# Recurrence loads with three and four buffers in place of five, and one load moved

## Chip, cores, metric

One core of a Trainium2 chip runs the whole program. The metric is device time in microseconds of one execution. Of the kernel before there are three timed runs and one profiled execution.

## What is computed

Three stages, each reading what the one before it wrote. Everything is float32 at the interface.

```python
def _attn_ref(r, k, v, w, u):            # (4, 8, 768, 48) each; w, u (8, 48)
    ...
    for t in range(S):
        kt, vt, rt = (k[:, :, t], v[:, :, t], r[:, :, t])
        cur = np.einsum('bhd,bhe->bhde', u[None] * kt, vt)
        y[:, :, t] = np.einsum('bhd,bhde->bhe', rt, state + cur)
        state = w[None, :, :, None] * state + np.einsum('bhd,bhe->bhde', kt, vt)
def _moe_ref(x, w_skip, w_gate, w1, w2):  # x: (3072, 384), 8 experts, hidden 1024
    ...                                   # tokens with x @ w_skip > 0 go to their best expert
    out[do_compute] = xc + gate_w * (relu(xc @ w1[e]) @ w2[e])
def _moe2_ref(x, phi, w1, w2):            # soft slots: 8 experts with 4 slots each
    ...
```

The change lies in the loads of the first stage, the recurrence.

## The kernel before

The recurrence is done in chunks: 768 steps are 6 chunks of 128, and a tile is one chunk of one of the 4 batches, all 8 heads. There are 24 tiles; tile j is chunk j // 4 of batch j % 4. Within a tile the recurrence is matmuls: scores of keys against queries (`scores`, L656), the scores times the values (`av`, L753, in two halves, the second of which is followed by a copy to `yt`, L758), the state's part (`inter`, L734), and the update of the state (`upd`, L679). The loop at L1024 runs over i, and tile i's scores stand beside the `av` of tile i - 1 and the transposes of tile i - 2.

Two loads feed a tile, both issued on the queue of SP (SyncE) by `load(j)`:

- `rk` (L514): r and k with the head dimension on the partitions, 112 partitions of 4 KB. Its readers are the three products of `prep(j)`: two on DVE (VectorE) at L635 and L636, one on POOL (GpSimd) at L638 (`pd`). The buffers `rkb` are a list of NRK = 5 fixed tiles; tile j uses number j modulo NRK.
- `kv` (L519): k and v with time on the partitions, 128 partitions of 3 KB. Its readers are `prepk(j)` on POOL (L644, the product `kt`, for tiles 0 to 19), then TensorE in `upd(j)` (L679, which reads `kt` and v) and in `av(j)` (L753). The tile `kvt` comes from a pool with five buffers in turn. A load into a buffer waits until the last reader of its former tile is done, which is the second half of `av`.

`prep(i + 1)` and `prepk(i + 1)` are issued in pass i, after the scores of tile i. The engines follow an order written out by hand: every engine, SP too, takes its instructions in the order of the program, so a load that waits holds all that stands behind it on SP. In pass i that is `load(i + 3)`, then from pass 20 to 22 two loads of expert weights each (`wload`, L966 and L968, 768 KB each), and every fourth pass a store of x (`stored`, L809); the last three stores come after the loop. The loads 0 to 2 are issued before the loop (L521 to L626), load 3 at the top of pass 0, ahead of `decays()`, `warm`, `prep(0)` and `prepk(0)`.

After the loop the routing of the tokens is finished, and POOL gathers the tokens of the first expert from the x in HBM with `idg` as the index (`gload`, L1197). The expert stage (`mm1` L1266 to L1269, `mm2` L1291 to L1293) follows, then the slots.

Of the kernel before, what the change touches and what calls it, by code (L numbers as in the profile page):

```python
# [8 lines left out]
F32 = mybir.dt.float32  # L9
# [10 lines left out]
P = 128  # L20
NC_ = S // P
NT = B * NC_
DM = H * D
# [451 lines left out]
def tile_main(ctx, tc, rk, kv, wu, wcat, phi, w1, w2, v1, v2, r_in, k_in, v_in, w_in, u_in, wcn, out, dbg=None, force=False):  # L475
# [9 lines left out]
    wk = ap.enter_context(tc.tile_pool(name="wk", bufs=2))  # L485
# [4 lines left out]
    PE_, DVE_, ACT_, POOL_, SP_ = (mybir.EngineType.PE, mybir.EngineType.DVE, mybir.EngineType.Activation, mybir.EngineType.Pool, mybir.EngineType.SP)  # L490
    mst = ExitStack()
    mst.enter_context(tc.manual_schedule(engines={PE_, DVE_, ACT_, POOL_, SP_}))
    NRK = 5
    ones = fp.tile([P, P], BF16, name="ones")
    nc.vector.memset(ones, float(E))

    def warm(n, w=P):

        wp = ps.tile([P, 2, 4 * P], F32, tag="y", name="wp")[:, 0, 0 : 4 * w]
        for _ in range(n):  # L500
            nc.tensor.matmul(wp, ones, ones[:, 0:w].rearrange("p (o n) -> p o n", o=1).to_broadcast([P, 4, w]), start=True, stop=True)  # L501

    warm(NWARM, 48)
    rkb = [kp.tile([PR, 2, 4, P], F32, name=f"rkb{i}") for i in range(NRK)]
    wt = kp.tile([PR, 2, 4], F32, name="wt")
# [4 lines left out]
    def load(j, first=True, last=True):  # L510
        c, b = divmod(j, B)
        if first:
            t = T[j] = {"rk": rkb[j % NRK]}
            nc.sync.dma_start(out=t["rk"], in_=rk[c, b])  # L514
        if not last:
            return
        t = T[j]
        t["kv"] = wk.tile([P, 2, DM], F32, tag="kvt", bufs=5, name=f"kvt{j}")
        nc.sync.dma_start(out=t["kv"], in_=kv[c, b])  # L519

    load(0, last=False)  # L521
    load(1, last=False)
    load(0, first=False)
    wcs = fp.tile([PR, 4, 64], F32, name="wcs")
    nc.scalar.dma_start(out=wcs, in_=wcat)
# [87 lines left out]
    def decays():  # L613

        pkp = ps.tile([P, 4, 128], F32, tag="r", name="pkp")
        for p in range(4):
            nc.tensor.transpose(pkp[:, p, 0:PR], pks[:, p, :], ident[:PR, :PR])
        to, fr = pktok.rearrange("t (p f) d -> t p f d", f=2), pkp.rearrange("t p (g d) -> t p g d", d=64)
        nc.scalar.copy(to[:, 2:4], fr[:, 2:4, :, 0:D])
        for g in range(2):  # L620
            nc.scalar.copy(to[:, 0:2, 1 - g], fr[:, 0:2, g, 0:D])
# [8 lines left out]
    def prep(j):  # L630
        t = T[j]
        rkt = t["rk"]
        rks = wk.tile([PR, 2, 4, P], F32, tag="rks", bufs=3, name=f"rks{j}")
        t["rs"], t["ks"] = rks[:, 0], rks[:, 1]
        nc.vector.tensor_mul(rks[:, 0], rkt[:, 0], prt)  # L635
        nc.vector.tensor_mul(rks[:, 1], rkt[:, 1], pkt)  # L636
        t["pd"] = wk.tile([PR, 4, P], F32, tag="pd", name=f"pd{j}")
        nc.gpsimd.tensor_mul(t["pd"], rkt[:, 0], rkt[:, 1])  # L638

    def prepk(j):  # L640
        t = T[j]
        if j < NT - B:
            t["kt"] = wk.tile([P, DM], F32, tag="kt", name=f"kt{j}")
            nc.gpsimd.tensor_mul(t["kt"], t["kv"][:, 0], pktok.rearrange("t h d -> t (h d)"))  # L644
# [377 lines left out]
    pa = Banks(u=[(ps, "t", 1)])  # L1022
    if True:
        for i in range(NT):  # L1024
            if i + 3 < NT:
                load(i + 3)
            rc, rb = divmod(i - 5, B)
            rok = 0 <= rc < NC_ - 1
            if i == 0:
                decays()  # L1030
                warm(5, 48)
                prep(0)
                prepk(0)
                for hf in range(2):
                    r0 = 64 * hf
                    nc.vector.tensor_copy(usel[r0 : r0 + D, :, hf : hf + 1], wt[r0 : r0 + D, 1, :].rearrange("p (a o) -> p a o", o=1))
# [318 lines left out]
    if True:  # L1355
# [4 lines left out]
        for n in range(NS + 1):  # L1360
# [12 lines left out]
            f = e - 1  # L1373
# [300 lines left out]
```

## Time and profile before

| | us |
|---|---|
| three timed runs | 348.92, 350.14, 354.14 |
| their median | 350.14 |
| the profiled execution | 348.07 |
| its span (first to last instruction) | 346.3 |
| mean granted clock of TensorE, share of full | 0.967 |

The profiled execution is the one that the rows below describe; what lies around its span is 1.8 us. PE is TensorE's matmuls, PEld its weight loads, SPq the queue of DMA issues on SP. A busy PE is not PE at its peak, since matmuls overlap. Times in rows are microseconds from the start of the span; a line number is that of the kernel before.

### The profile page before, as it was taken

The numbers are of one execution on the slowest core, as the hardware profiler recorded it, in microseconds if no ns is written. First come the engines' busy times: TensorE is split into PE (matmuls) and PEld (weight loads), VectorE is DVE, ScalarE is ACT, GpSimd is POOL, SyncE is SP. The second block draws the span as 40 slices with busy tenths as digits, with TensorE's granted clock in tenths as the row PEclk, the third lists the DMA queues.
The fourth block names the chain that finished last, engine by engine and source line by source line (L and its number), as shares of the span: only waits on it lengthen the run. The fifth ranks groups of instructions, "written<-read, shape, count | busy, mean of one in ns | idle before, by whom it ended". The sixth has DMA issues, their size and how long they took to land.

```text
span 346.3 us, 10440 instructions
## 1 busy us (share of the span) xinstructions
PE 321.4 (93%) x4326; PEld 263.9 (76%) x4326; DVE 226.1 (65%) x510; ACT 159.5 (46%) x353; POOL 139.8 (40%) x181
## 2 busy tenths in 40 slices
PE   8699998999998999999999999999999999999950
PEld 8477776767775782999999999998999998534540
DVE  6637676896969865776675848575676845226850
ACT  3235454444543463554645546464645543121360
POOL 3939685776844544804324232525224002200000
PEclk9969999999999998999999999999999999899995
DMA  7976667684879944899788787878866749779096
GB/s 233 287 220 190 187 189 255 199 269 141 279 191 310 387 163 158 266 310 315 252 288 303 239 281 255 263 257 296 294 197 215 254 124 377 256 268 324 10 338 210
DMA packets 45735, 85.29 MB, mean 246 GB/s; under 512 B 3838, under 2 KB 26672, under 8 KB 45680
## 3 DMA queue, kind: packets, MB, share of 16 engines
q1 hardware_dynamic: 43024, 80.63, 70.8%
q0 software_dynamic: 2128, 3.74, 3.9%
q8 instruction: 36, 0.59, 0.7%
q10 hardware_dynamic: 528, 0.16, 0.2%
q14 instruction: 19, 0.16, 0.1%
HBM read 74.49 MB, written 10.10 MB: 244 GB/s over the span
## 4 chain that ended last, share of the span: by engine, by line
PE 79%; DVE 12%; issue 3%; ACT 2%; POOL 1%; ACTq 0%; DVEq 0%
PE yp L1291 7%; PE yp L1292 6%; PE yp L1293 6%; PE hp L1266 6%; PE hp L1269 6%; PE hp L1267 6%; PE yp L753 4%; PE ehp L216 4%; PE sc L656 3%; PE lgt L837 3%; PE ud L679 3%; PE trp L764 3%; PE yp L734 2%; PE wp L501 2%; PE ud L666 2%
## 5 line engine op out<-in xcount | busy, mean ns | idle before, releaser
L1266 PE MATMUL hp<-xhl,wa 128*128 128x240 f32 x192 | 46.1, 282 | 0.2 <-issue 0.2
L1291 PE MATMUL yp<-wb,hh 128*128 128x384 f32 x128 | 45.2, 353 | 0.0
L1004 DVE TENSOR_TENSOR wa<-w,wa 128x768 fp32r<-128x768 f32 x32 | 30.5, 955 | 22.4 <-ACT wa L1016 22.3
L1267 PE MATMUL hp<-xhl,wa 128*128 128x240 f32 x192 | 44.6, 275 | 0.0
L1292 PE MATMUL yp<-wb,hh 128*128 128x384 f32 x128 | 43.0, 336 | 0.0
L1293 PE MATMUL yp<-wb,hl 128*128 128x384 f32 x128 | 42.9, 335 | 0.0
L1197 POOL DMA_INDIRECT xg<-x_d,idg x16 | 19.9, 1242 | 51.9 <-DVE x L1299 38.1
L638 POOL TENSOR_TENSOR pd<-rkb 112x512 f32<-112x512 f32 x24 | 31.1, 1295 | 18.6 <-PE ud L666 15.3
L1321 POOL DMA_INDIRECT lt_d<-lsr,ids x16 | 17.7, 1106 | 50.2 <-ACT xhl L1256 28.3
L1266 PEld LDWEIGHTS hp<-xhl,wa 128*128 128x128 f32 x192 | 36.2, 189 | 0.5 <-ACT dsbv L135 0.5
L1267 PEld LDWEIGHTS hp<-xhl,wa 128*128 128x128 f32 x192 | 36.2, 189 | 0.0
L714 DVE COPY_PREDICATED at<-ih,ud 128x512 f32<-128x512 int32 x24 | 17.7, 738 | 26.0 <-ACT us L695 16.5
L1004 DVE TENSOR_TENSOR wb<-w,wb 128x768 fp32r<-128x768 f32 x32 | 30.5, 953 | 2.1 <-ACT wb L1016 1.7
L1016 ACT CAST wb<-w 128x768 fp32r<-128x768 f32 x32 | 26.8, 838 | 9.5 <-PE yp L1293 5.5
L753 PE MATMUL yp<-at,kvt 64*48 64x64 f32 (+3 forms) x800 | 27.7, 250 | 1.0 <-DVE at L714 0.4
L1276 ACT ACTIVATE hh<-hp 128x480 fp32r<-128x480 f32 x32 | 18.3, 572 | 22.2 <-PE hp L1269 20.0
L1277 DVE SCALAR_TENSOR_TENSOR hl<-hp,hh 128x480 fp32r<-128x480 f32 x32 | 20.9, 654 | 9.7 <-ACT hh L1276 9.2
L1016 ACT CAST wa<-w 128x768 fp32r<-128x768 f32 x32 | 26.9, 840 | 0.0
L1291 PEld LDWEIGHTS yp<-wb,hh 128*128 128x128 f32 x128 | 24.0, 188 | 3.6 <-issue 3.5
L1269 PE MATMUL hp<-xhl,wa 128*128 128x240 f32 x192 | 26.7, 275 | 0.0
L656 PE MATMUL sc<-rks 48*64 48x128 f32 (+1 forms) x768 | 22.1, 252 | 4.5 <-DVE at L705 2.3
L753 PEld LDWEIGHTS yp<-at,kvt 64*48 64x48 f32 (+1 forms) x800 | 22.2, 125 | 5.3 <-issue 1.6
(346 smaller groups left out, 697.1 us busy)
## 6 DMA issues: line engine op xcount, KB each, us to landing
w<-in_w_dram SPq DMA_DIRECT2D x32, 768.0 KB
v<-in_v_dram SPq DMA_DIRECT2D x29, 768.0 KB
rkb<-in_rk_dram SPq DMA_DIRECT2D x24, 448.0 KB
kvt<-in_kv_dram SPq DMA_DIRECT2D x24, 384.0 KB
x_d<-x SPq DMA_DIRECT2D x5, 768.0 KB
out_dram<-ob SPq DMA_DIRECT2D x5, 768.0 KB
x<-in_v_dram SPq DMA_DIRECT2D x2, 768.0 KB
x_d<-x SPq DMA_DIRECT2D x2, 384.0 KB
```

The lines of the kernel that those rows point to most:

```text
L638: nc.gpsimd.tensor_mul(t["pd"], rkt[:, 0], rkt[:, 1])
L656: nc.tensor.matmul(sc[c0 : c0 + HT, g, blocks(p, z), :], ks[r0 : r0 + D, p, HT * z : HT * z + HT], rs[r0 : r0 + D, p, HT * z :], start=Tru ...
L753: nc.tensor.matmul(d, kvt[s0 : s0 + HT, 1, h * D : h * D + m], w, start=(c == ph == z == 0), stop=(ph == z == 1))
L1004: nc.vector.tensor_sub(lv, sl, hv.bitcast(F32))
L1016: nc.scalar.copy(hv, sl)
L1266: nc.tensor.matmul(hp[:, f, 0:ROOM], hi[:, k, fs], xh[:, k, 0:ROOM], start=(k == 0 and f == 0), stop=False)
L1267: nc.tensor.matmul(hp[:, f, 0:ROOM], lo[:, k, fs], xh[:, k, 0:ROOM], start=False, stop=False)
L1269: nc.tensor.matmul(hp[:, f, 0:ROOM], hi[:, k, fs], xl[:, k, 0:ROOM], start=False, stop=(k == 2 and f == 1))
L1277: nc.vector.scalar_tensor_tensor(l, p, 0.0, h.bitcast(F32), op0=ALU.max, op1=ALU.subtract)
L1291: nc.tensor.matmul(YP[e][bl], hh[:, f, bs], hi[:, f, :], start=st, stop=False)
L1292: nc.tensor.matmul(YP[e][bl], hh[:, f, bs], lo[:, f, :], start=False, stop=False)
L1293: nc.tensor.matmul(YP[e][bl], hlo[:, f, bs], hi[:, f, :], start=False, stop=en)
```

## The change

NRK goes from 5 to 3, the pool's buffers for `kvt` from 5 to 4, and load 3 moves from the top of pass 0 to behind `prep(0)` and `prepk(0)`, which read tile 0. The other loads stay where they are. Since `load(i + 3)` stands at the top of pass i, the `rk` of tile i + 3 takes the buffer that `prep(i)` read in the pass before, and its `kv` takes the buffer of tile i - 1, whose last reader, `av(i - 1)`, comes later in the same pass.

```diff
-    NRK = 5
+    NRK = 3
...
-        t["kv"] = wk.tile([P, 2, DM], F32, tag="kvt", bufs=5, name=f"kvt{j}")
+        t["kv"] = wk.tile([P, 2, DM], F32, tag="kvt", bufs=4, name=f"kvt{j}")
...
         for i in range(NT):
-            if i + 3 < NT:
+            if 0 < i < NT - 3:
                 load(i + 3)
...
                 prep(0)
                 prepk(0)
+                load(3)
```

## Rows read from the trace of the kernel before

**Rows 1.** The page: busy us by engine, with share of the span and instructions.
```profile
PE 321.4 (93%) x4326; PEld 263.9 (76%) x4326; DVE 226.1 (65%) x510; ACT 159.5 (46%) x353; POOL 139.8 (40%) x181
```

**Rows 2.** Busy time in the recurrence: stretch, length, PE, PEld, DVE, ACT, POOL, clock, DMA, GB/s.
```profile
23.40:125.40 102.00, 96.29 (x2380) 72.96 (x2373) 77.75 (x200) 48.06 (x128) 66.68 (x88) 1.00 0.75 238
```

**Rows 3.** Waits of SP's queue, longest first: us in total, times, longest.
```profile
SPq L519 <- PE yp L753: 68.9, 19, 6.8
```

**Rows 4.** Waits of PE over the whole span: the longest in total.
```profile
PE sc L656 <- DVE at L705: 2.3, 5, 0.9
```

**Rows 5.** SP's issues in order of time: start, us, line (two stretches).
```profile
27.27 0.33 SPq L519 DMA_DIRECT2D kvt<-in_kv_dram  x1
31.19 0.33 SPq L519 DMA_DIRECT2D kvt<-in_kv_dram  x1
31.62 1.20 SPq L514 DMA_DIRECT2D rkb<-in_rk_dram  x1
...
80.50 0.33 SPq L519 DMA_DIRECT2D kvt<-in_kv_dram  x1
```

**Rows 6.** Busy time in the stretches behind kv issues (last number: GB/s).
```profile
31.20:34.50 3.30, 3.29 (x94) 2.55 (x86) 3.06 (x10) 1.80 (x5) 2.51 (x4) 1.00 0.71 194
80.50:84.50 4.00, 3.96 (x105) 3.21 (x101) 3.48 (x5) 2.05 (x6) 2.94 (x5) 1.00 0.67 214
```

**Rows 7.** POOL in order of time: kt of tile 7, pd of tile 8.
```profile
34.50 1.01 POOL L644 TENSOR_TENSOR kt<-kvt,pktok 128x384 f32<-128x384 f32 x1
...
37.20 1.27 POOL L638 TENSOR_TENSOR pd<-rkb 112x512 f32<-112x512 f32 x1 [0.67 <-PE ud L666]
```

**Rows 8.** PE in order of time: the update of tile 7.
```profile
43.63 0.67 PE L679 MATMUL ud<-kvt,kt 128*64 128x48 f32 x16
```

**Rows 9.** POOL's groups from 23.4 to 125.4: busy, mean ns, idle before, releasers.
```profile
L644 POOL TENSOR_TENSOR kt<-kvt,pktok 128x384 f32<-128x384 f32 x15 | 15.1, 1006 | 6.6 <-PE ud L679 6.6
```

**Rows 10.** SP's issues at the start: rk 3, kv 6.
```profile
4.36 0.43 SPq L514 DMA_DIRECT2D rkb<-in_rk_dram  x1
...
22.95 0.33 SPq L519 DMA_DIRECT2D kvt<-in_kv_dram  x1
```

**Rows 11.** DVE and POOL in order of time: readers of tiles 0 and 5.
```profile
7.34 0.68 DVE L636 TENSOR_TENSOR rks<-rkb,prt 112x512 f32<-112x512 f32 x1
...
26.68 1.00 POOL L644 TENSOR_TENSOR kt<-kvt,pktok 128x384 f32<-128x384 f32 x1
```

**Rows 12.** Busy time in stretches of the start.
```profile
0.00:8.00 8.00, 6.87 (x53) 6.61 (x53) 5.08 (x20) 2.22 (x6) 3.32 (x15) 1.00 0.76 217
...
8.00:14.50 6.50, 5.51 (x153) 4.07 (x154) 4.68 (x10) 2.22 (x9) 5.93 (x14) 1.00 1.04 299
...
17.30:23.40 6.10, 6.10 (x109) 5.01 (x112) 1.70 (x3) 1.92 (x5) 2.27 (x2) 0.50 0.79 208
```

**Rows 13.** SP's issues at the end of the recurrence: last kv, last x store.
```profile
103.80 0.33 SPq L519 DMA_DIRECT2D kvt<-in_kv_dram  x1
...
128.30 0.36 SPq L809 DMA_DIRECT2D x_d<-x  x1
```

**Rows 14.** ACT in order of time: yt of tiles 19 and 20.
```profile
107.21 0.59 ACT L758 COPY yt<-yp 112x512 f32<-112x512 f32 x1 [0.39 <-PE yp L753]
...
113.94 0.59 ACT L758 COPY yt<-yp 112x512 f32<-112x512 f32 x1 [0.32 <-PE yp L753]
```

**Rows 15.** Busy time in stretches of the hand-over.
```profile
122.00:126.00 4.00, 4.00 (x89) 3.42 (x88) 2.18 (x12) 2.17 (x7) 1.81 (x3) 1.00 0.58 211
126.00:129.00 3.00, 2.74 (x58) 2.67 (x57) 2.79 (x14) 1.83 (x7) 1.30 (x2) 1.00 0.00 0
```

**Rows 16.** DVE and POOL in order of time: index and first gather.
```profile
132.14 0.17 DVE L1174 CAST idg<-idp 128x16 int32<-128x16 f32 x1 [1.75 <-PE idp L815]
...
133.68 1.28 POOL L1197 DMA_INDIRECT xg<-x_d,idg  x1 [4.46 <-DVE c4v L979]
```

**Rows 17.** PE in order of time: the scores of tile 2, second part.
```profile
17.30 1.01 PE L656 MATMUL sc<-rks 48*64 48x64 f32 x19 [2.22 <-issue]
```

## Prediction

> **What bounds the kernel now.** I read the page's engine line first: PE (TensorE) is busy 93% of a span of 346.3 us, every other engine 65% or less [rows 1]. Then the busy time of the stage that the change touches: in the recurrence (23.4 to 125.4 us) PE is busy 96.3 of 102 us at full clock, while the DMA engines are busy 0.75 of the time [rows 2]. The reader is to see that PE sets the pace here too, and that a load costs time only if PE or its feeders wait for it. So the third view is who waits. The DMA queue of SP (SyncE) stands 68.9 us at the k-and-v load, in 19 waits, for TensorE's last reading of an older tile (L753) [rows 3]. PE's own list is another matter: its longest entry is 2.3 us for DVE (VectorE) over the whole span, and no load is in the list [rows 4]. SP's 68.9 us are the slack of a prefetch, not a loss.
>
> **What the change does to the loads.** There are two kinds of load per tile: rk (448 KB, L514) and kv (384 KB, L519), in one queue, in the order kv j, rk j+1. Counting the issues, the kv load at 27.27 us is tile 7's, the next (31.19) tile 8's, and each comes as TensorE finishes the tile five back [rows 5]. With four buffers kv j waits for tile j-4 instead: tile 7's load takes the moment that tile 8's has now. So from tile 5 on each kv load, and the rk load queued behind it, is issued one tile later, and the queue shows the same rows with the tile number lowered by one. The wait of rk itself (three buffers: the products of tile j-3, which run about a tile ahead of TensorE) is over long before the wait in front of it. Nothing is added or removed: 24 loads of each kind, the same bytes, the same instructions on every compute engine. The 11 KB per partition set free (two buffers of 4 KB, one of 3 KB) are taken by nothing in the diff.
>
> What it costs follows from three spans of tile 7, the tile with least to spare.
>
> 1. Issue to landing. After the issue at 31.19 the DMA engines move 194 GB/s x 3.3 us = 640 KB until 34.5 [rows 5, 6]. The 384 KB (393,000 bytes) of kv go ahead of the rk behind them: at the latest they are in by 34.5, at the earliest, at that rate and with nothing between, after 2.0 us, at 33.2.
>
> 2. First reader. POOL (GpSimd) starts kt of tile 7 at 34.50 us [rows 7]. So in the new order the data come in 0 to 1.3 us before kt wants to start, and that is all that is left of a tile's 4 us of lead.
>
> 3. Second reader. TensorE wants kt of tile 7 (L679) at 43.63 us [rows 8], and kt ends at 34.50 + 1.01 = 35.51. There are 8.1 us between. POOL is ahead because what it waits for is TensorE: all 6.6 us of idle time before its kt products are put down to the previous L679 [rows 9].
>
> So even a load late by 2 us moves kt into idle time of POOL. The cover is those 8 us; were it gone, 1 us of delay in each of some 16 tiles would be 16 us. The rk loads get the same shift: rk 8 would be issued where rk 9 is now (31.62) and the pair is in within 4.0 us of the kv issue (80.50 to 84.50 moves 214 GB/s x 4.0 us = 856 KB, all of both loads) [rows 5, 6]; its first reader, pd of tile 8, starts at 37.20 [rows 5, 7]. Cost of the steady part: 0 us; bounds: 0 below, because after the first tiles no engine waits for these loads now and none can gain from them, and 7.5 us above, if the cover of item 3 is not there (C). I take 0, since item 3 is the row nearest to the wait in question.
>
> **The start.** Load 3 moves behind prep(0), whose last reading of rk 0 is DVE's at 7.34 + 0.68 = 8.02 us; now rk 3 is issued at 4.36 [rows 10, 11]. But the DMA engines are full anyway from 8 to 14.5 us (share 1.04, 299 GB/s) [rows 12]. Up to 8 us some 1.7 MB have been moved (217 GB/s), and tiles 0 to 2 are 2.56 MB, so at 299 GB/s there is work in the queue until about 10.8 us, some 2.8 us after the late issue of rk 3. The order of the transfers stays, and nothing starves: 0 us. The first load that is shifted in steady order is kv 5: it goes out at 22.95, where kv 6 goes now, 3.7 us before kt of tile 5 at 26.68 [rows 10, 11], more than the 3.3 us of tile 7.
>
> **The end of the recurrence.** Behind the last load stand, on SP, six weight loads and the stores of x, which the gathers of the expert stage need. The last kv load goes out at 103.80, the moment at which TensorE finishes tile 18; it will go out as tile 19 is copied off, at 107.21 [rows 13, 14]. The weights shift by 3.4 us. They and the stores of x fill the queue to 126 us, at 211 GB/s in its last 4 us; then follow 3.0 us with no byte until the last store, issued at 128.30 [rows 13, 15]. A shift of 3.4 us fills that hole, and may run over it by 0.4 us; some of the 122 to 126 stretch is slack too (844 KB in 4 us, 2.8 us at the 299 GB/s of the start). The gather of the first expert starts at 133.68, while its index is ready at 132.14 + 0.17 [rows 16]; whether the store or the index lets it go, the rows don't show. I take +0.3 us, the run-over nearly whole; bounds 0 and +3 (below).
>
> **Sum.** 0 + 0 + 0.3 us on the profiled execution, which took 348.07 us (span 346.3 and 1.8 around it) [rows 1], gives 348.4. The median of the three runs shown is 350.14, 2.07 above it, so as a median: 350.4 us. Within 2% is about what a measurement of this kernel can tell from no change.
>
> **Rivals.**
>
> [...]
>
> *B, slower at the hand-over to the experts.* The mechanism is the one store queue: the x stores stand behind the weights. If the weights shift not by 3.4 us but by a long tile (the next copy of yt comes at 113.94, 6.7 us after 107.21) [rows 14], the hole of 3.0 us and some 0.7 us of the slack before it are used up and the gather comes 3.0 us late: 350.1 + 3.0 = 353.1. It decides from a shift of about 3.7 us. For it: the margin is small. Against it: the waited-for reading is named in the rows, and it is that of tile 19.
>
> *C, slower throughout.* If kt comes so late that TensorE meets it, the same gap returns with every tile. If TensorE had to stand for half of each kt product, 0.5 of its 1.0 us, the 15 products of [rows 9] would make 7.5 us: 357.9. For it: item 2 leaves nearly nothing. Against it: item 3. [...] In this trace SP shows the same gap tile after tile, and PE, the engine in question, none.
>
> *D, the loads don't shift:* SP is held at the same moments as now by something later than the older tile's last reading; 350.1. For it: nothing in SP's waits [rows 3]. Time can't tell it from the forecast; the rows of SP can.
>
> **How the numbers follow.** Forecast with D 0.72, A 0.10, B 0.09, C 0.09. The forecast's own range is the spread of the runs shown, 348.1 to 354.1 us, and it takes in B. Reaching down to A gives 345.1 to 354.1; C stays outside. Faster by over 2% (below 343.1) needs all of A and the low end of the runs' spread: 0.04. Slower by over 2% (above 357.1) is most of C: 0.08. Same: 0.88.
>
> **What would show it.** Right: SP's wait at the kv load stays near 70 us and its rows lie at the same times, one tile lower; kt's idle time before it is still put down to L679, with at most a microsecond or two to the kv load; PE's list has no load in it; the hole in the transfers at 126 to 129 is closed or nearly; the first gather starts within 0.5 us of its old time relative to the index. Wrong: a wait of PE for kt or for a load in every tile (C), a gather that waits for x stores (B), or a start without the 2.2 us of "issue" and at full clock (A).

## The result, and the profile after

The changed kernel takes 345.16 us in the median of 22 runs, the kernel before 349.37 us in 22 runs beside it. The ratio is 0.9909, with a 95% interval of 0.9881 to 0.9937: 0.9% faster, some 3.2 us, where no change was forecast. The ratio leaves out the slower runs of either kernel, so it lies nearer to 1 than the quotient of the two medians (0.988). The profiled execution of the changed kernel (span 348.3 us) is one of its longer runs; its rows show what happens in which order, and the gain has to be read from many runs.

The page of the changed kernel: busy time of PE, and the granted clock in 40 slices of the span.

```profile
PE 322.0 (92%) x4326; PEld 264.6 (76%) x4326; DVE 228.2 (66%) x510; ACT 159.7 (46%) x353; POOL 139.9 (40%) x181
...
PEclk9959999999999999999999999999999999699995
```

As in [rows 1], PE is what is busy. The third slice of the clock (17.4 to 26.1 us) is at half: in this execution the stretch of [rows 12] at clock 0.50 is there, and longer than before (from 15.93 to 26.17 us, 10.2 us, against 6.8 from 16.54 to 23.36).

The waits of the changed kernel, of SP's queue and of PE: total us, times, longest.

```profile
SPq L519 <- PE yp L753: 68.6, 18, 6.7
...
PE sc L656 <- DVE at L705: 4.7, 6, 2.5
PE sc L656 <- issue: 2.8, 1, 2.8
```

SP stands as long as in [rows 3], once less. PE's list has no load in it, but the wait for DVE has grown from 2.3 us [rows 4] to 4.7, with one of 2.5; it comes up again below.

SP's issues in order of time, changed kernel: start, us, line.

```profile
8.02 0.33 SPq L514 DMA_DIRECT2D rkb<-in_rk_dram  x1
8.39 0.43 SPq L519 DMA_DIRECT2D kvt<-in_kv_dram  x1
10.83 0.33 SPq L514 DMA_DIRECT2D rkb<-in_rk_dram  x1
14.68 0.33 SPq L519 DMA_DIRECT2D kvt<-in_kv_dram  x1
15.11 1.46 SPq L514 DMA_DIRECT2D rkb<-in_rk_dram  x1
23.38 0.33 SPq L519 DMA_DIRECT2D kvt<-in_kv_dram  x1
...
109.53 0.33 SPq L519 DMA_DIRECT2D kvt<-in_kv_dram  x1
```

The same queue of the kernel before, from 7 to 16 us:

```profile
7.35 0.33 SPq L519 DMA_DIRECT2D kvt<-in_kv_dram  x1
8.29 0.33 SPq L514 DMA_DIRECT2D rkb<-in_rk_dram  x1
14.86 0.33 SPq L519 DMA_DIRECT2D kvt<-in_kv_dram  x1
15.29 0.77 SPq L514 DMA_DIRECT2D rkb<-in_rk_dram  x1
```

These are kv 4, rk 5, kv 5 and rk 6. In the changed kernel rk 3 goes out at 8.02 in place of 4.36; kv 4 and rk 5 go out at 14.68 and 15.11, when kv 5 and rk 6 did; the kv load at 23.38 is tile 5's (at 22.95 it was tile 6's) [rows 10], and the last kv load goes out as tile 19 is copied off [rows 13, 14].

POOL's group of kt products from 23.4 to 125.4 us, changed kernel: busy, mean ns, idle before them and its releasers.

```profile
L644 POOL TENSOR_TENSOR kt<-kvt,pktok 128x384 f32<-128x384 f32 x15 | 15.0, 1003 | 7.4 <-PE ud L679 5.5 <-DMA kvt<-in_kv_dram 1.9
```

The load is now what POOL waits for in 1.9 us, against none in [rows 9].

Busy time in two stretches of the hand-over, changed kernel (last numbers: clock, DMA share, GB/s), and then its index and first gather on DVE and POOL.

```profile
124.00:128.00 4.00, 4.00 (x91) 3.46 (x89) 1.93 (x10) 2.11 (x7) 2.08 (x4) 1.00 1.06 394
128.00:131.50 3.50, 3.24 (x64) 3.10 (x67) 3.22 (x17) 2.33 (x8) 1.51 (x2) 1.00 0.56 206
```

```profile
133.16 0.17 DVE L1175 CAST idg<-idp 128x16 int32<-128x16 f32 x1 [0.50 <-PE idp L815]
...
134.51 1.28 POOL L1198 DMA_INDIRECT xg<-x_d,idg  x1 [3.01 <-DVE cmax L1208]
```

The hole of [rows 15] is filled (394 and 206 GB/s where there were 3 us with no byte), and the gather starts 1.35 us behind the start of the index, 1.54 in [rows 16].

### The profile page after: what moved, and what is told of

Same layout as the page of the kernel before. It is cut to its first block, busy times and chain, and to the rows that moved or that the text cites. A ratio compares the mean times of both kernels' runs of the same rounds, so it can differ in the third digit from the quotient of the medians.

```text
span 348.3 us, 10443 instructions
## 1 busy us (share of the span) xinstructions
PE 322.0 (92%) x4326; PEld 264.6 (76%) x4326; DVE 228.2 (66%) x510; ACT 159.7 (46%) x353; POOL 139.9 (40%) x181
## 4 chain that ended last, share of the span: by engine, by line
PE 72%; DVE 17%; issue 3%; ACT 2%; DMA 2%; POOL 1%; SPq 0%; DVEq 0%; ACTq 0%; POOLq 0%
PE yp L1292 7%; PE yp L1293 6%; PE yp L1294 6%; PE hp L1267 6%; PE hp L1270 6%; PE hp L1268 6%; PE ehp L216 4%; PE yp L753 3%; PE lgt L837 3%; DVE at L714 2%; PE sc L656 2%; PE ud L679 2%; PE trp L764 2%; DMA kvt<-in_kv_dram 2%; PE xtp L1255 2%
## 5 line engine op out<-in xcount | busy, mean ns | idle before, releaser
L656 PE MATMUL sc<-rks 48*64 48x128 f32 (+1 forms) x768 | 22.5, 255 | 7.7 <-DVE at L705 4.7
L1277 ACT ACTIVATE hh<-hp 128x480 fp32r<-128x480 f32 x32 | 18.3, 572 | 22.1 <-PE hp L1270 21.4
L656 PEld LDWEIGHTS sc<-rks 48*64 48x64 f32 x768 | 19.6, 139 | 9.4 <-DVE at L705 5.7
```

The source lines that it names most:

```text
L656: nc.tensor.matmul(sc[c0 : c0 + HT, g, blocks(p, z), :], ks[r0 : r0 + D, p, HT * z : HT * z + HT], rs[r0 : r0 + D, p, HT * z :], start=Tru ...
```

## Where the time went: a first reading over many runs

Over 109 runs of the kernel before (e1 and those beside the experiments) and 35 of the changed one, the means are 349.55 and 346.49 us (standard errors 0.23 and 0.52), the mean spans 347.8 and 344.6, the mean granted clocks 0.9646 and 0.9704. If the clock is either full or half, the time at half is 2 x (1 - clock) x span: 24.6 us before, 20.4 after. (In the profiles of both kernels the granted clock is 1.00 or 0.50 throughout.) If each such microsecond costs a half, which is an estimate for stretches in which PE is busy (in the profile of the kernel before the 16 matmuls of L679 take 1.09 us at clock 0.50, from 20.51, and 0.64 at 1.00, from 25.77, so that 0.41 of each microsecond is lost there), 2.1 of the 3.1 us are clock and 1.0 us is other time, with standard errors of 0.45 and 0.3. The question became where the half clock is spared.

## The experiments

### The two kernels again, and each edit alone

e1 is the kernel before, e2 the changed kernel, both as they are. e3 has only the move of load 3, e4 only the four buffers, e5 the three buffers with the move they need.

```diff
# e3
-            if i + 3 < NT:
+            if 0 < i < NT - 3:
...
+                load(3)
# e4
-        tag="kvt", bufs=5
+        tag="kvt", bufs=4
# e5: e3, and
-    NRK = 5
+    NRK = 3
```

> The kernel before once more, to see which of its stages vary from one execution to the next. Both theories: ratio 1.000 within 0.4%. Theory S (the gain of 0.9% lies in the first 25 us, where the queue of loads is shorter): PE again stands 2 us or more with issue near 15 to 17 us and then runs 6.8 us or more at half clock. Theory H (the gain lies at the hand-over from the recurrence to the experts, 125 to 140 us): half clock again for 3.4 us there, and 14 us from the last yt copy to the first expert matmul.

> The changed kernel once more, for a profile of an undisturbed execution. Both theories: ratio 0.991 within 0.4%. Theory S: the half clock of the start is shorter than 6.8 us, or the scores of tile 4 start before 26.9 us. Theory H: the start as in the kernel before (scores of tile 4 at 27 us), and no half clock between 125 and 140 us, 1.7 us gained there.

> Only load 3 moves behind the readers of tile 0; five buffers for both loads as before. Theory S: half of the gain or more, ratio 0.993 to 0.996, because the queue is shorter at the start. Theory H: 1.000, because the loads, weights and stores from tile 5 on go out at the old times. If a load three places back in the queue costs nothing, 1.000 in any case.

> Only the k-and-v load has four buffers in place of five; load 3 stays at the top of the loop and r-and-k keeps five. From tile 4 on every load and the expert weights go out one tile later. Theory H: all of the gain, ratio 0.991. Theory S: the loads of tiles 5 and 6 are out of the queue between 15 and 23 us here too, so most of it, 0.992 to 0.996, with the start faster; the stage in which the time is gained tells the two apart.

> Three buffers for r and k and the fourth load behind the first tile's reading, but five buffers for k and v as before. From the third-stage loads on, r-and-k loads then wait for the products of the tile three back, and the k-and-v loads queued behind them wait too in the first tiles. Theory Q (a shorter queue of loads in the first 25 us is what gains, whichever buffers make it short): most of the changed kernel's gain, about 346.5 us, 2 to 4 us below the kernel before. Theory M (the memory set free, 11 KB per partition, lets the tiles of the expert stage start apart from the recurrence's): part of it at most, since 8 KB are free here and the gathers' buffers still lie over the recurrence's last tiles; 348 to 350 us. Theory K (both counts are needed): 349.5 us, as with either edit alone.

Medians: e1 349.6 us, e2 346.1, e3 349.4, e4 349.2, e5 349.7, beside 349.6 for the kernel before (350.4 beside e5). By ratio none of these five is apart from 1 by itself: e2 is 0.9965 with an interval of 0.9914 to 1.0015, e4 0.9961 with 0.9911 to 1.001, e5 0.9964 with 0.9918 to 1.001. So these runs alone don't part the single edits from the changed kernel. But no single edit shows the changed kernel's median, nor its clock: 0.9644, 0.9656 and 0.9642 for e3, e4 and e5, against 0.9704. e3 could not have shown anything: its rk 3 still goes out at 4.36 us, as in [rows 10]. With five buffers nothing holds the load: it goes out at 4.36 us though its call stands behind the readers of tile 0, the last of which ends at 8.02 in the kernel before [rows 11]. It is the count of three that holds it (8.02 us in the changed kernel). For e5, theory Q's 346.5 us did not come; the time is theory K's.

### Cut behind the hand-over, and the freed memory filled

e6 and e7 are the kernels before and after, ended in front of the experts' loop. e8 is the changed kernel with three tiles that nobody uses in the place of the freed buffers.

```diff
# e8
+    room = [kp.tile([PR, 2, 4, P], F32, name=f"room{i}") for i in range(2)]
...
+    roomv = wk.tile([P, 2, DM], F32, tag="roomv", bufs=1, name="roomv")
```

> The kernel before, ended behind the hand-over to the experts (first gathers, first expert's sums); the experts' loop, the second mixture and the output are left out, and one small block is stored. About 150 us. To be set against the changed kernel cut at the same place. Theory Q: the cut changed kernel is 2 to 4 us shorter than this one, since the whole gain arises before this point. Rival L (the gain arises in the experts' loop, by the phase of the half-clock stretches there): the two differ by less than 1 us.

> The changed kernel, ended behind the hand-over to the experts as the run beside it; the experts' loop, the second mixture and the output are left out. Theory Q: 2 to 4 us below the cut kernel before. Rival L: within 1 us of it.

> The changed kernel with the 11 KB per partition that it sets free filled by three unused tiles, so that every other tile of the program lies where it lies in the kernel before, and the expert stage's tiles lie over the same tiles of the recurrence. Theory Q: as the changed kernel, about 346 us. Theory M: the gain is gone, about 349.6 us.

e6 takes 149.2 us, e7 144.9 (six runs each; 147.3 to 151.3 and 143.9 to 146.5, so that no run of one is as short as the longest of the other). The whole gain is there before the experts' loop, and rival L falls. The cut kernels even differ by 4.3 us; whether the loop gives 1 us of that back isn't shown. Mean clocks are 0.9347 and 0.9600. Taken off the mean spans by the sum above, the half clock leaves 137.9 and 137.7 us: in the cut kernels the gain is clock and nothing else that can be seen, to within about 1 us. (Some 11 us of each kernel's half clock is its end, where PE has next to no work: 10.5 in e6's profile, 11.2 in e7's.) e8 takes 345.5 us (ratio 0.9859, 0.9798 to 0.9919): the gain is there with the memory filled, and theory M's 349.6 is not.

The cut lies behind the hand-over, so it does not tell theory H (the gain at the hand-over) from S. Four buffers for k and v alone do. In e4 the last kv load, and with it the weights and stores behind it, goes out later than the 103.80 us of [rows 13]:

```profile
108.31 0.33 SPq L519 DMA_DIRECT2D kvt<-in_kv_dram  x1
```

The shift at the hand-over is there, but e4's 349.2 us (ratio 0.9961) don't show the 0.991 that theory H gave it, and the cut kernel with these buffers (e9, below) takes 149.9 us, not less than e6's 149.2. Theory H falls.

What is spared shows in the stretch from 18 us. First e6, then e7: stretch, length, PE, PEld, DVE, ACT, POOL, clock, DMA share, GB/s.

```profile
18.00:25.00 7.00, 5.86 (x127) 4.54 (x126) 2.38 (x4) 2.39 (x6) 2.92 (x3) 0.76 0.91 227
```

```profile
18.00:25.00 7.00, 6.56 (x196) 5.27 (x198) 4.04 (x7) 3.77 (x9) 4.90 (x7) 1.00 0.50 149
```

The same 7 us give 127 matmuls in e6 and 196 in e7, with the DMA engines busy 0.91 and 0.50 of the time. PE in order of time, first e6, then e7, where a row's idle time in front is put down to "issue":

```profile
18.69 0.96 PE L656 MATMUL sc<-rks 48*64 48x64 f32 x19 [2.81 <-issue]
...
26.57 0.54 PE L753 MATMUL yp<-at,kvt 64*64 64x128 f32 x10 [1.94 <-issue]
```

```profile
16.06 0.61 PE L656 MATMUL sc<-rks 48*64 48x64 f32 x19 [1.17 <-issue]
...
20.80 0.54 PE L753 MATMUL yp<-at,kvt 64*64 64x128 f32 x10 [0.28 <-issue]
```

The first is the place at which [rows 17] has its 2.22 us. In every profile that has it this stall ends at the same matmul, the 221st of PE's program (in order of time), some 1.5 us after the end of a transfer of 16 KB in the queue that the trace calls "instruction". All later stalls of over 0.6 us put down to "issue", in any profile up to 80 us, end at the 348th, 474th, 1111th, 1239th, 1366th or 1620th matmul: steps of 126 to 128 or a multiple of 127, as a program read in equal pieces would have them. So I read "issue" here as PE without code, an inference from these counts and times. The DMA queues of e6 in two stretches, then of e7 in one: packets, MB, share of 16 engines.

```profile
q1 hardware_dynamic: 630, 1.59, 97.2%
...
q8 instruction: 1, 0.02, 23.6%
```

```profile
q1 hardware_dynamic: 64, 0.21, 83.4%
q8 instruction: 1, 0.02, 7.6%
```

In e6 the loads (q1) fill the engines from 17.5 to 23.9 us without one packet of code, and the code (q8) starts at 24.0, behind the last packet of kv 5 (23.9). In e7 it starts at 18.25, among the loads of 17.5 to 18.4.

### Theory C: code behind loads

Of the next four runs, cut like e6 and e7, e9 and e10 split the two buffer counts; e11 takes loads out of the queue at the start, and e12 adds two. The kernel before took 347.7 us beside these four and 350.4 beside e6 and e7.

```diff
# e9, against e7
-    NRK = 3
+    NRK = 5
# e10, against e7
-        tag="kvt", bufs=4
+        tag="kvt", bufs=5
# e11, against e7
-            nc.sync.dma_start(out=t["rk"], in_=rk[c, b])
+            if j not in (3, 4, 5):
+                nc.sync.dma_start(out=t["rk"], in_=rk[c, b])
# e12, against e6
                 load(i + 3)
+            if i == 1:
+                wload(0)
...
-            if 20 <= i < 23:
+            if 20 < i < 23:
                 wload(i - 20)
```

> Ended behind the hand-over like the two cut kernels of the last runs (149.2 us before, 144.9 us changed; the experts' loop, the second mixture and the output are left out). Here the fourth tile's load is behind the first tile's reading and k and v have four buffers, but r and k keep five. Theory C (TensorE's next 16 KB of code is fetched late behind the loads that are in the queue at 10 to 16 us; what counts is how many of them have been issued by then): the issues up to 16 us are nearly the changed kernel's, so 144.5 to 146 us, with a gap of 1 to 2 us at 15 us. Rival N (the count of three for r and k does it, by holding a load back until the products of the tile three back): 148 to 150 us.

> Cut as the others (the experts' loop, the second mixture and the output are left out). Three buffers for r and k and the late fourth load, but five buffers for k and v. The uncut kernel of this kind showed no stall at 15 us, one of 1.75 us at 52 us, and 349.7 us. Theory C: no stall at 15 us, but more loads under way from 16 us on than in the changed kernel, so later fetches of code come late: 146 to 149 us. Rival N: 144 to 146 us.

> The changed kernel, cut as the others, without the loads of r and k of the fourth, fifth and sixth tile: these tiles' products are made of the older tiles' data (left out: 1.3 MB of loads, the experts' loop, the second mixture and the output). The DMA engines then have little to do between 12 and 15 us. Theory C: the fetch of code starts before 13 us, TensorE's stall at 15 us is gone (under 0.5 us) and there is no half clock before 60 us: 142.5 to 144 us. Rival P (the stall is TensorE's own, not from the loads): the stall stays at 1.2 to 2.8 us and the time at 144.9 us or above.

> The kernel before, cut as the others (the experts' loop, the second mixture and the output are left out), with the first expert weights' two loads (1.57 MB) moved from the end of the recurrence to behind the fifth tile's loads, so that more stands in the load queue from 9 us on; the data of the next tiles still come in time for TensorE. Theory C: the fetches of code at 14 and 20 us start later than before, the stall at 15 us grows beyond 3 us or a second one appears, half clock until 25 us or more: 150 to 154 us. Rival T (the DMA engines take turns between the queues, so the length of the load queue does not matter): 149 us, as the cut kernel before, or less, since the weights no longer stand in the queue at the hand-over.

e11 takes 144.25 us, with four runs from 143.5 to 144.3 and two of 147.2 and 150.8. Its queues from 9 to 12.6 us, and its stretches from 12 and 18 us:

```profile
q1 hardware_dynamic: 453, 0.88, 71.0%
q8 instruction: 1, 0.02, 1.6%
```

```profile
12.00:18.00 6.00, 5.38 (x157) 4.04 (x147) 4.82 (x8) 2.47 (x7) 5.55 (x14) 1.00 0.23 65
18.00:25.00 7.00, 6.85 (x199) 5.42 (x195) 5.01 (x9) 3.87 (x11) 5.07 (x8) 1.00 0.56 179
```

The first fetch starts at 11.56 us (13.3 to 16.0 in all other profiles), no stall before 60 us is over 0.6 us, and the clock is full to the end of the recurrence. Rival P falls: where the loads are gone, so is the stall. The time lies between the two ranges, 0.25 us above theory C's and below P's, and two long runs of six (clocks of 0.944 and 0.929, against 0.955 to 0.967 in the four) say that these loads are not all that can bring the half clock.

e12 takes 151.85 us, 2.7 above e6, within 150 to 154; rival T, which gave 149 or less, falls. Theory C had part of it wrong: the first two fetches start no later than in the kernel before (14.5 and 21.2 us), and the stall at 15 us did not grow (2.26). A second stall came further on, at the 474th matmul, where e6 has none (its second, of 1.94 us, is at the 348th); PE in order of time, and the load queue from 24 to 29.15 us:

```profile
31.83 0.55 PE L679 MATMUL ud<-kvt,kt 128*48 128x48 f32 x13 [2.85 <-issue]
```

```profile
q1 hardware_dynamic: 440, 1.40, 104.2%
```

The code for it started at 29.15 us, behind 5 us of a full load queue.

e9 takes 149.9 us and misses theory C's 144.5 to 146. What failed is what I took for granted of its issues, the same mistake as in e3: rk 3, kv 3 and rk 4 go out at 4.2, 5.7 and 6.1 us, not at 8.0, 8.4 and 10.3 as in e7. e10 takes 150.5, in no theory's range (146 to 149, and 144 to 146). The table sets the profiles side by side, sorted by the buffer counts; times in us.

| profile | rk / kv buffers | first fetch | stall at its end | second fetch | half clock before 65 us |
|---|---|---|---|---|---|
| before | 5 / 5 | 14.5 | 2.2 | 21.7 | 6.8 |
| e1 | 5 / 5 | 14.8 | 2.6 | 22.5 | 17.1 |
| e3 | 5 / 5 | 14.1 | 2.0 | 20.3 | 6.8 |
| e6 | 5 / 5 | 16.0 | 2.8 | 24.0 | 3.4 |
| e4 | 5 / 4 | 15.5 | 3.1 | 19.6 | 10.2 |
| e9 | 5 / 4 | 14.7 | 1.8 | 18.7 | 6.8 |
| e5 | 3 / 5 | 13.4 | none | 19.1 | 6.8 |
| e10 | 3 / 5 | 15.4 | 2.3 | 23.3 | 6.8 |
| after | 3 / 4 | 14.9 | 2.8 | 19.3 | 10.2 |
| e2 | 3 / 4 | 13.9 | 1.4 | 18.6 | 10.2 |
| e7 | 3 / 4 | 13.5 | 1.2 | 18.3 | 0 |
| e16 (as e7) | 3 / 4 | 13.3 | none | 19.1 | 0 |
| e8 | 3 / 4 | 13.7 | 1.5 | 18.4 | 0 |
| e11, loads left out | 3 / 4 | 11.6 | none | 16.1 | 0 |

The buffers for k and v act on the second fetch. With four buffers for k and v the second fetch starts at 18.3 to 19.6 us, with five at 19.1 to 24.0: kv 5 and rk 6, which the fifth buffer lets go at 15 us, are then in front of it. (Two later runs with four, e13 and e17, have 20.2 and 20.5.) Counted from the 221st matmul, so that the first stall is out of it, it starts 1.3 to 2.2 us later with four (3.4 in e16, and 3.8 and 2.8 in e13 and e17) and 2.9 to 5.3 with five. It starts within 1.0 us of the last packet of kv 4 in the seven profiles with four (e11 apart), and within 1.1 us of the last packet of kv 5 in five of the six with five (e5: 2.2 ahead of it).

With three buffers for r and k the first fetch starts at 13.3 to 15.4, with five at 14.1 to 16.0; the difference is small against the spread, so what the three buffers do is not shown by it. The first fetch starts within 1.2 us of the last packet of kv 3 in every profile of this study (e6: 16.4; e7: 13.5; e11: 11.6), and that packet comes at its own time in each execution, so two profiles of one kernel differ (the fetch is at 14.9 us in the profile of the changed kernel, at 13.9 in e2). The profiles of the table without half clock have both fetches early, by 13.7 and 19.1 us. Two entries of the last column begin elsewhere: e5's 6.8 us at 54.4 us, behind a later stall, and 3.4 of e2's 10.2 at 36.9, behind a wait of PE for DVE.

The four profiles with five and five buffers have a mean stall of 2.4 us and 8.5 us of half clock, the five with three and four (e11 apart) 1.4 and 4.1. That is 1.0 us of stall and, at a half, 2.2 of clock, near the 1.0 and 2.1 of the many runs; but single profiles differ by more than that, and e1 alone gives half of the 8.5.

### What was still open: the second fetch alone, and a stall given back

e15 is e10 without the loads of rk 5 and 6. e13 and e14 (cut) take small operations off VectorE, and e16 is e7 once more beside them.

```diff
# e15, against e10
-            nc.sync.dma_start(out=t["rk"], in_=rk[c, b])
+            if j not in (5, 6):
+                nc.sync.dma_start(out=t["rk"], in_=rk[c, b])
# e13, e14, against the changed kernel
-            nc.vector.tensor_scalar(w8, eb_i, ...
+            nc.gpsimd.tensor_scalar(w8, eb_i, ...
...
-            if i == 4:
+            if i == 2:
                 odd = ...
                 tf = ...
-                nc.vector.tensor_scalar(tj[:, 0], ...
-                nc.vector.tensor_sub(tj[:, 1], ...
+            if i == 4:
+                nc.gpsimd.tensor_scalar(tj[:, 0], ...
+                nc.gpsimd.tensor_sub(tj[:, 1], ...
```

> The changed kernel with three small operations of the fifth tile's set-up (the two that write tj, and w8) moved from VectorE to GpSimd, and what they read computed two tiles earlier. Theory G (in the changed kernel kt of tile 6 waits for its load, so that GpSimd's products fall beside VectorE's small operations and these stand until a product ends; the changed kernel loses part of its gain there): the stall of 1.4 to 2.5 us at 31 to 38 us is gone from the profile, and the median is 1 to 2 us below the changed kernel's 346, about 344.5 us. Rival U (the stall is rare without the profiler, or comes back elsewhere): within 0.7 us of the changed kernel.

> The same edit in the cut kernel (the experts' loop, the second mixture and the output are left out). Theory G: 143 to 144.2 us, 1 to 2 us below the cut changed kernel beside it. Rival U: within 0.7 us of it.

> Three buffers for r and k and five for k and v, cut as the others, and without the loads of r and k of the sixth and seventh tile (left out: 0.9 MB of loads, the experts' loop, the second mixture and the output). The loads that are in the queue between 14 and 19 us are then those of k and v alone. Theory C (the fetches of code stand behind the loads issued before them): the second fetch starts at 17 to 19 us in place of 19 to 23.3, no stall at 20 to 25 us, and 145 to 147.5 us against 150.5 with these loads. Rival V (five buffers for k and v cost by themselves, wherever the loads lie): 150 us.

> The cut changed kernel once more, on the chip of the two runs above. All theories: 144 to 146 us, as before; its profile adds a further look at the start: a stall of 1 to 2.8 us at 15 us, and by theory G a small VectorE operation beside GpSimd's products at 29 to 36 us in some executions.

e15 has its second fetch at 17.9 us, 2.0 us behind the 221st matmul, and no stall at 20 to 25, as theory C said. Its time, 149.4 us, is rival V's. PE in order of time of e15 shows a stall that is in e5 (1.75 us) and, smaller, in e10 (0.94), before (0.68) and e3 (0.66) as well, and in e15 half clock follows it at 52.5:

```profile
52.34 0.77 PE L735 MATMUL yp<-rks,sp 48*48 48x128 f32 x10 [1.20 <-issue]
```

The 16 KB in front of that stall started at 49.6 us in e15 and 51.3 in e5, against 48.0 in e7 and 48.6 in e16. So e5 and e15 pay at a later fetch, and I can't say why that one comes late; the half clock of e10's profile starts at 17.1 us, behind the first. The sums without the half clock show it too: 139.8 us in e10 and 139.4 in e15, 137.7 in e7 and 138.3 in e16.

The new wait of PE in the changed kernel comes from here; DVE, then POOL in order of time, and then DVE of e16:

```profile
33.90 2.15 DVE L1123 TENSOR_TENSOR tj<-tf,tj 128x24 bf16<-128x24 f32 x1
```

```profile
33.79 1.27 POOL L638 TENSOR_TENSOR pd<-rkb 112x512 f32<-112x512 f32 x1
35.02 0.99 POOL L644 TENSOR_TENSOR kt<-kvt,pktok 128x384 f32<-128x384 f32 x1
```

```profile
29.98 0.18 DVE L1123 TENSOR_TENSOR tj<-tf,tj 128x24 bf16<-128x24 f32 x1
```

An operation of 0.18 us lasts 2.15, until the second of POOL's products is through; PE waits 2.5 us for what DVE does next. In e2 it is 2.16 us (PE waits 2.4, and 3.4 us of half clock follow), in e8 1.22 (1.4), in e17 0.18. In the profile of before these products lay elsewhere, and here POOL had stood 0.7 us for kv 6 first. Moving the operations off DVE removed the stall from the profile of e13, but its time is 345.8 us in 12 runs (0.9928, 0.988 to 0.9977), and e14's is 146.8 beside e16's 145.9. Theory G's 1 to 2 us are not there; rival U holds. The stall is real in the rows, and its share in the mean time was not found.

### Shifting the place in the program

```diff
# e17, e18 (cut), against the changed kernel
-    warm(NWARM, 48)
+    warm(16)
```

> The changed kernel with TensorE's warm-up made of 16 matmuls of 128x512 in place of 44 of 128x192 (8192 columns in place of 8448, about the same time), so that every later matmul stands 28 places earlier in TensorE's program. Theory C (the first late fetch starts when the loads issued before it are in, at 13.3 to 14.9 us, whatever the place in the program): the code in hand now lasts 28 matmuls longer, some 1.5 us (to about 16.5 us), the stall at 15 us is under 1 us, and the median 0.5 to 2 us below the changed kernel's 346. Rival W (the fetch is asked for at a place in the program, so it moves along with it): the stall stays at 1 to 2.8 us, 28 matmuls later, and the time at 346 within 0.7 us.

> The same edit in the cut changed kernel (the experts' loop, the second mixture and the output are left out), to be set against its 144.9 and 145.9 us. Theory C: 143.5 to 144.8 us, no stall above 1 us before 25 us. Rival W: 144.9 to 146 us.

The fetch did not move with the program: it starts at 15.0 us in e17 (last packet of kv 3 at 16.2) and 13.8 in e18 (14.6). PE now runs 28 matmuls further on the code it has, to 16.1 us in e17:

```profile
17.73 0.34 PE L753 MATMUL yp<-at,kvt 64*64 64x64 f32 x8 [1.60 <-issue]
```

e18 has no stall there. So the place of the stall is what theory C said, and its size in e17 is not (under 1 us was expected). The times are rival W's, and one is worse: 346.5 us for e17 (0.9917, 0.9885 to 0.995), 148.3 for e18 with runs from 144.7 to 153.7. Nothing tried beats the changed kernel beyond its uncertainty.

## Why the prediction was wrong

The forecast of 350.4 us missed; the measured median lies at the lower end of the range, where rival A stood with a chance of 0.10.

- **The steady loads** went as forecast: rows at the same times with the tile number lowered by one, only from kv 4 and rk 5 on and not from kv 5; kt still released by L679, 1.9 us of kt's idle time at the load, and no load in PE's list. The cover of 8 us held, and C did not come. What was not seen is that the lost lead shifts POOL against DVE.
- **The end of the recurrence** went as forecast as well: the weights shift by one copy of yt, the hole is filled, the gather is 1.35 us behind the index in place of 1.54. It is let go by DVE, not by the stores, so B did not come, and the term of +0.3 us is not there.
- **The start** is the step that failed: "The order of the transfers stays, and nothing starves: 0 us." No tile starves, but PE's code comes late behind the same loads (the first fetch at 16.03 us in e6, at 11.56 in e11). In place of 0 the runs gave -3.1 us, by the estimate above 2.1 of it half clock spared and 1.0 other time. The cut kernels place it ahead of the experts' loop, and the profiles at the fetches up to 25 us.
- **Rival A**, faster at the start, named the mechanism. By its estimate a shorter queue of loads, without kv 5 and rk 6, spares PE the 2.22 us of "issue" [rows 17] and half of the 6.10 us at clock 0.50 [rows 12], 5.3 us in all, which gives 345.1 us. The argument against it, that at 14.5 us the transfers under way are those of tiles 3 and 4 in both orders and only what lies behind them is gone, holds for the stall in [rows 17], which is still 1.2 to 2.8 us in most profiles of the changed kernel (none in e16), though kv 4 is not even issued in the new order before 14.68 us. It missed the next fetch, some 5 us later, in front of which kv 5 and rk 6 were. No run shows A's 5.3 us, from which the range has its lower end of 345.1: -2.2 us of stall and -3.1 of clock were too large on both terms, where the runs gave 1.0 us of other time and 2.1 of clock by the estimate above. That 345.1 is the measured median is in part luck of the scale, since the kernel before measured 349.4 and not 350.1.
- **D** fell: the loads do shift.

Shown by runs: that the gain lies ahead of the experts' loop (e6, e7) and not at the hand-over (e4, e9), that it is mostly clock, that both counts are needed (medians of 149.9 and 150.5 us in e9 and e10, of 144.9 and 145.9 in e7 and e16), that it does not need the memory set free (e8), and that taking loads out of the queue takes the stall away and adding loads brings a further one (e11, e12). Argued from single profiles only: that the spared half clock is that behind the first two fetches. Not settled: what the three buffers for r and k do, why the cut kernels with three and five lose (e10, e15, the latter with both fetches early), and how the 1.0 us of other time divides.

## What to carry to other kernels

Where PE stands on "issue", look for the 16 KB transfers of the instruction queue before calling it noise, and count the loads that were issued ahead of them: a prefetch deeper than the data need can cost code (two loads more, 1.57 MB, brought a second stall of 2.85 us in e12). Early in this kernel fewer buffers were worth more than the slack that they gave up, and what followed a stall at half clock could cost as much as the stall or more (in the kernel before 6.8 us at half behind 2.2). A load moved in the program was not moved in time where nothing held it (rk 3 at 4.36 us in the kernel before and in e3): read its issue row first.

## What the runs showed of the hardware

The first fetch of code came some 4.5 us later with the loads than without: at 16.03 us in e6, at 11.56 in e11, where PE is as far (its first scores at 8.96 and 8.85 us; 220 matmuls had started by the fetch in e6, 118 in e11). From 12 to 18 us the DMA engines moved 250 GB/s at a share of 1.04 in e6, 65 GB/s at 0.23 in e11. How they divide their time between the queue of the loads and that of the code no run here tells. When the fetch is asked for, no row shows.

The granted clock fell to 0.50 during PE's stalls for code or up to 1.4 us behind them: with every one of 2.0 us and more, and with some of the shorter: behind 1.41 us in e2, not behind 1.46 in e8 or the second stall in e6 (1.94).

A VectorE operation of 24 elements a partition lasted 0.18 us alone (in the profile of the kernel before from 32.75, where POOL rests until 33.27), 1.22 beside one GpSimd product (e8) and up to 2.16 beside two. In the profile of the changed kernel tj<-tf,tj starts at 33.90 us, inside POOL's pd (33.79 to 35.06), and ends at 36.05, with POOL's kt (35.02 + 0.99 = 36.01); in e8 it runs from 29.80 to 31.02, beside pd alone (29.72 to 30.98). So it ended with a GpSimd product in both, and in the first, where a second product followed, it lasted through that one as well. Why, no row shows.
